# Gated mix of linear attention and a squared-ReLU layer: the query weights folded in one wide burst instead of two narrow ones

## The chip, the cores and the metric

The kernel runs on one core of a Trainium2 chip. The metric is the time of one execution on the device, in microseconds (us). TensorE (PE in the profile) multiplies matrices out of SBUF into eight PSUM banks of 128 x 512 floats; VectorE (DVE), ScalarE (ACT) and GpSimd (POOL) do the element-wise work; SyncE (SP) issues transfers, as GpSimd and ScalarE also do.

## The reference

2048 tokens of width 512, 32 heads of 16, a hidden layer of 1792. Per head the queries and keys go through a small 16x16 matrix `w_phi` and a pair of softmaxes; the attention is linear; its output is mixed by a gate with that of a feed-forward layer:

```python
pq = einsum("bhsd,hdf->bhsf", q, w_phi)          # pk alike from k
phi_q = concat([softmax(pq), softmax(-pq)], -1)  # phi_k alike
kv  = einsum("bhsf,bhsd->bhfd", phi_k, v)
z   = einsum("bhsf->bhf", phi_k)
num = einsum("bhqf,bhfd->bhqd", phi_q, kv)
den = einsum("bhqf,bhf->bhq", phi_q, z)[..., None] + 1e-6
a   = (num / den).transpose(...) @ wo
b   = relu(x @ w1 + b1) ** 2 @ w2 + b2
out = g * a + (1 - g) * b                        # g = sigmoid(sum(x * gate_w))
```

## The kernel before

Every large product is made of three TensorE instructions (`mm3`, L74 to L78): both operands are split into a high and a low part, and high x high, high x low and low x high are added in one bank. The splits (`split`, L61) are a copy on ScalarE (L63) and a subtraction on VectorE (L66).

The work is a list of 56 items (L848), 28 in each of two sweeps. An item is one of the 7 hidden tiles of a sweep for one of the 4 blocks of 512 tokens: twelve products "up" (tile `u`, first layer, into one bank), ScalarE's and VectorE's work on it (`hidden`, L422: relu L425, square L427, split into `hh` and `hl`), and twelve products "down" into four banks `d0` to `d3`, which hold a block's sums over seven items and are then read by VectorE (`gated`, L449). The up of an item is issued two items ahead of its down. The first sweep's partial outputs go to DRAM on GpSimd's queue (L910).

Between these products stands everything else, at places given by slots (`at`, L790): an item has two slots, and half slots lie in the middle of its up and its down. In the first sweep eight pairs of key and value chunks are worked (`pair_steps`, L660, at slot 14 + 4.5 p for pair p): products `pX` and `pY` (L656 to L658), read by ScalarE (L675) and VectorE (L677), the softmaxes (`exps`, L300), and at last the sums over tokens (`kv_chunk`, L323), bursts of small products into the bank `kvps`, which holds them from the first pair to the last. In the second sweep the queries are projected (`do_q`), made into features (`q_phi`, L340), turned and placed by transfers (`transposed`, L361: L363 and L372), and multiplied with the sums (`numer`, L384, `num`) and with `wo` (`attended`, `att`).

Besides `d0` to `d3` there are four banks (`ps_a`, `ps_b`, `ps_e`, `ps_f`). `bank` (L53) hands them out in turn to `u`, `pY`, the folds and the query phase; `ps_b` is out of the turn while it is `kvps`, and `ps_e` while it is `pX`.

The small matrix `w_phi` is not applied to queries but to the weights: `query_fold` multiplies the query weights by it on the chip. The weights come transposed (`wqT`, four rows of 128 x 512, `load_fold`, L141), the small matrices as 32x32 blocks of two heads. `query_fold(half)` (L191) runs at slots 51.5 and 53, near the end of the first sweep: 32 products of a 32x32 block with 128 columns into two banks (64 records in the trace, two to a product). VectorE turns each bank in 32x32 squares (L174) into the tile `turned`, and ScalarE and VectorE split it into `wqh` and `wql`, which `q` (from slot 56.5) reads. The same is done for the keys at the start, with four banks in one burst (`tiles_fold`, L177).

The framework sets each engine's order from the order of the code and from priorities (`high_priority`) and explicit orders (`issue_after`). Within an engine instructions run in that order, and an instruction that waits holds up what is behind it.

## Time and profile before

| | |
|---|---|
| time, median of 3 runs | 506.5 us (506.25 to 506.56) |
| profiled execution | 506.27 us, of which the span of its instructions is 504.5 us |
| PE busy | 499.7 us, 99% of the span |
| VectorE, ScalarE, GpSimd busy | 404.7, 259.9 and 88.1 us |
| mean granted clock of TensorE | 0.999 |
| data moved | 76.13 MB, 151 GB/s on average |

How to read it: times in rows of a timeline are the start, in us from the start of the span, and the duration; "x4" groups instructions that follow each other. Products on PE overlap: a row of 0.39 us is followed by the next start 0.23 us later, so a stretch of PE is measured from start to start. In brackets stands the idle time of the engine ahead of an instruction, with what ended it. Names are those of the program, without buffer numbers: `d`, `u`, `fold`, `num`, `pX`, `pY`, `kvps` are banks.

### The profile page before, as it was taken

To read this page: it belongs to the slowest core of one execution; us is meant where nothing else is said; L and a number is where in the kernel's file an instruction comes from. 1 tells how busy PE (TensorE), PEld (TensorE's weight loads), DVE (VectorE), ACT (ScalarE), POOL (GpSimd) and SP (SyncE) were. 2 spreads that over 40 slices of the span, in tenths; PEclk is the share of its full clock that TensorE was granted. 3 is DMA by queue.
4 is the path that set the end of the run, shared out by engine and by line. 5 is a ranking of instruction groups with operands and counts; after the bars stand their busy time and mean duration, and the time that the engine had idled before them with its cause. 6 is when DMAs were issued, how large, how long until landed. Compare 5 with 4: busy or idle time off the path is not lost.

```text
span 504.5 us, 9559 instructions
## 1 busy us (share of the span) xinstructions
PE 499.7 (99%) x3616; PEld 403.9 (80%) x3616; DVE 404.7 (80%) x680; ACT 259.9 (52%) x470; POOL 88.1 (17%) x103
## 2 busy tenths in 40 slices
PE   8999999999999999999999999999999999999997
PEld 5878788888888888888788878788787878788776
DVE  5569957799785969796988989897979796897724
ACT  4887655466263474453793644454455353333540
POOL 1000151204510025000012140212222221112200
PEclk9999999999999999999999999999999999999999
DMA  8858587666854578762167131324212221041112
GB/s 263 285 197 279 184 315 215 215 216 233 295 187 156 180 225 309 261 218 75 43 182 280 39 109 47 101 71 138 54 31 90 71 88 44 6 136 51 36 29 83
DMA packets 45830, 76.13 MB, mean 151 GB/s; under 512 B 6869, under 2 KB 23001, under 8 KB 45785
## 3 DMA queue, kind: packets, MB, share of 16 engines
q1 hardware_dynamic: 36072, 41.78, 26.5%
q10 hardware_dynamic: 6768, 23.79, 13.6%
q0 software_dynamic: 2944, 9.96, 5.4%
q8 instruction: 28, 0.46, 0.3%
q14 instruction: 18, 0.14, 0.1%
HBM read 57.68 MB, written 11.54 MB: 137 GB/s over the span
## 4 chain that ended last, share of the span: by engine, by line
PE 93%; DMA 3%; DVE 2%; issue 1%; ACT 1%; SPq 0%; ACTq 0%; DVEq 0%
PE d L76 9%; PE d L77 9%; PE d L78 9%; PE u L76 9%; PE u L77 9%; PE u L78 9%; PE pX L656 3%; PE q L78 3%; PE att L78 3%; PE att L76 3%; PE q L76 3%; PE att L77 3%; PE q L77 3%; PE pX L658 3%; PE pX L657 3%; PE pY L656 2%
## 5 line engine op out<-in xcount | busy, mean ns | idle before, releaser
L425 ACT ACTIVATE r<-u,b1c 128x512 f32<-128x512 f32 x56 | 38.5, 687 | 110.1 <-PE u L78 108.3
L76 PE MATMUL d<-w2h,hh 128*128 128x512 f32 x222 | 86.8, 391 | 0.0
L77 PE MATMUL d<-w2l,hh 128*128 128x512 f32 x222 | 86.4, 389 | 0.0
L78 PE MATMUL d<-w2h,hl 128*128 128x512 f32 x222 | 86.4, 389 | 0.0
L76 PE MATMUL u<-xh,w1h 128*128 128x512 f32 x212 | 83.5, 394 | 0.0
L77 PE MATMUL u<-xl,w1h 128*128 128x512 f32 x212 | 82.6, 390 | 0.0
L78 PE MATMUL u<-xh,w1l 128*128 128x512 f32 x212 | 82.5, 389 | 0.0
L337 POOL TENSOR_TENSOR ez<-e,z 128x512 f32<-128x512 f32 x32 | 43.0, 1366 | 164.1 <-ACT e L313 164.1
L66 DVE TENSOR_TENSOR hl<-r,hh 128x512 fp32r<-128x512 f32 x56 | 37.9, 677 | 22.9 <-ACT hh L63 22.9
L76 PEld LDWEIGHTS d<-w2h,hh 128*128 128x128 f32 x222 | 41.7, 188 | 9.6 <-issue 1.0
L76 PEld LDWEIGHTS u<-xh,w1h 128*128 128x128 f32 x212 | 39.8, 188 | 11.4 <-issue 2.9
L78 PEld LDWEIGHTS d<-w2h,hl 128*128 128x128 f32 x222 | 41.7, 188 | 8.7
L77 PEld LDWEIGHTS d<-w2l,hh 128*128 128x128 f32 x222 | 41.7, 188 | 8.5
L78 PEld LDWEIGHTS u<-xh,w1l 128*128 128x128 f32 x212 | 39.8, 188 | 8.4
L77 PEld LDWEIGHTS u<-xl,w1h 128*128 128x128 f32 x212 | 39.8, 188 | 8.0
L313 ACT ACTIVATE e<-e 128x1024 f32<-128x1024 f32 x27 | 28.6, 1060 | 32.5 <-DVE e L311 32.1
L295 DVE TENSOR_REDUCE sm<-e 128x64 f32<-128x1024 f32 x27 | 32.8, 1215 | 10.8 <-ACT e L313 10.8
L63 ACT ACTIVATE hh<-r 128x512 fp32r<-128x512 f32 x56 | 35.1, 627 | 1.0
L427 ACT ACTIVATE r<-r 128x512 f32<-128x512 f32 x56 | 34.9, 624 | 0.7
L378 ACT ACTIVATE phiT<-tb 32x256 f32<-32x256 f32 x64 | 26.4, 413 | 8.8 <-DVE tb L363 7.9
L695 ACT ACTIVATE tmp<-pX 128x512 f32<-128x512 f32 x24 | 14.4, 598 | 29.7 <-PE pX L658 24.7
L347 DVE TENSOR_REDUCE dz<-ez 128x64 f32<-128x1024 f32 x16 | 19.4, 1212 | 11.7 <-POOL ez L337 11.7
(181 smaller groups left out, 981.4 us busy)
## 6 DMA issues: line engine op xcount, KB each, us to landing
sloto<-wkeep ACTq DMA_DIRECT2D x30, 512.0 KB, 4.3
in<-in_xT SPq DMA_DIRECT2D x42, 256.0 KB, 4.4
slotez<-wkeep ACTq DMA_DIRECT2D x15, 512.0 KB, 6.0
phiT<-tb SPq DMA_DIRECT2D x192, 32.0 KB, 1.8
in<-in_w SPq DMA_DIRECT2D x23, 256.0 KB, 3.3
part<-row POOLq DMA_DIRECT2D x16, 256.0 KB, 5.2
row<-part SPq DMA_DIRECT2D x16, 256.0 KB, 3.2
out<-row SPq DMA_DIRECT2D x15, 256.0 KB, 2.2
```

Source lines behind the costliest of these rows:

```text
L63: i = nc.scalar.activation(hi, src, AF.Copy)
L66: st["lo"] = elo.tensor_tensor(lo, src, hi.bitcast(F32), ALU.subtract)
L76: nc.tensor.matmul(o, ah[:, sa], bh[:, sb], start=first, stop=False)
L77: nc.tensor.matmul(o, ah[:, sa], bl[:, sb], start=False, stop=False)
L78: return nc.tensor.matmul(o, al[:, sa], bh[:, sb], start=False, stop=last)
L295: nc.vector.tensor_reduce(sm, e3, AX.X, ALU.add)
L313: nc.scalar.activation(ef, ef, AF.Exp)
L337: nc.gpsimd.tensor_tensor(ez[:, hs, :], e3[:, hs, :], zbc[half], ALU.mult)
L378: nc.scalar.activation(dst, src, AF.Copy)
L425: st["relu"] = nc.scalar.activation(r, ps, AF.Relu, bias=b1c[:, fc:fc + 1])
L427: nc.scalar.activation(r, r, AF.Square)
L656: nc.tensor.matmul(ps, h, wh, start=first and j == 0, stop=False, skip_group_check=True)
```

## The change

`query_fold` runs once, at slot 49.5, with all four banks: sixteen products of a 32x32 block with 512 columns, one for each pair of row group r (which has its own bank) and column group g. Its weights are loaded from slot 46. ScalarE copies the four banks to two tiles `cp` in eight instructions, VectorE turns each `cp` at once (128 x 1024), and sixteen transfers of 32 x 512 put the head groups where the splits want them (tiles `wq`), eight on SyncE's queue and eight on GpSimd's. The splits (`query_split`) follow at slots 52 and 52.5.

So that four banks are free by then, the sums of keys and values are cut in two: pairs 0 to 6 are read out at slot 48.5 (`kv_most`) by four ScalarE copies and `ps_b` goes back into the turn; pair 7 gets a bank of its own, its last products of `pY` come half a slot earlier, its sums a slot earlier, and GpSimd adds the two parts (`kv_done`). The sums and the rows made from them lie in tiles of the value phase that are no longer used. `kv_most` also sets a flag by which the split of one hidden tile gets a high priority. In the query phase the low parts of one block of x move from VectorE to GpSimd, and the work of the first pair gets priority.

```diff
-    def query_fold(half):
-        pss = {r: bank(f"fold{r}") for r in (2 * half, 2 * half + 1)}
-        for g, c, r in [(g, c, r) for g in range(NK) for c in range(4) for r in pss]:
...
-        part_ = lambda t: t.rearrange("p (g r f) -> p g r f", g=NK, f=32)[:, :, 2 * half:2 * half + 2, :]
+    def query_fold():
+        pss = [bank(f"fold{r}") for r in range(4)]
+        wph, *t = st["wT"]
+        for g in range(NK):
+            for r in range(4):
+                rows, cols = slice(32 * r, 32 * r + 32), slice(32 * g, 32 * g + 32)
...
+                        t[g][rows, :].rearrange("p (k c q) -> p c k q", c=4, q=32),
+                        start=True, stop=True, skip_group_check=True)
+        piece = lambda u, nm: work.tile([P, 2 * D], F32, tag=f"o{u}", name=nm, bufs=1)
+        part_ = lambda t: t.rearrange("p (c k r q) -> p c k r q", c=2, k=NK, q=32)
+        cps = [piece(u, "cp") for u in range(2)]
+        for u, cp in enumerate(cps):
+            for r in range(4):
+                with tc.high_priority(offset=AHEAD):
+                    nc.scalar.activation(
+                        part_(cp)[:, :, :, r, :],
+                        pss[r][:, 256 * u:256 * u + 256].rearrange("p (c k q) -> p c k q", c=2, q=32), AF.Copy)
+        tbs = [work.tile([P, 2 * D], F32, tag="tb", name="turned", bufs=2) for _ in range(2)]
+        for cp, tb in zip(cps, tbs):
+            with tc.high_priority(offset=AHEAD):
+                nc.vector.transpose(tb, cp)
+        st["wq"] = [piece(u, "wq") for u in range(2)]
+        for u, w in enumerate(st["wq"]):
+            for c in range(4):
+                for g in range(2):
+                    (nc.sync, nc.gpsimd)[c % 2].dma_start(
+                        w[32 * c:32 * c + 32, 512 * g:512 * g + 512],
+                        tbs[c // 2][32 * (2 * u + g):32 * (2 * u + g) + 32, 512 * (c % 2):512 * (c % 2) + 512])
+
+    def query_split(u):
+        part_ = lambda t: t.rearrange("p (g x) -> p g x", g=NK)[:, 2 * u:2 * u + 2, :]
         for k in range(NK):
-            if not half:
+            if not u:
                 st.setdefault("wa", []).append(tuple(
                     wpool.tile([P, 512], F32R, tag=f"wa{hl}{k}", name=f"wq{hl}{k}") for hl in "hl"))
             hi, lo = st["wa"][k]
-            split(tb[:, :, :, k].rearrange("p r g q -> p g r q"), part_(hi), part_(lo), nc.scalar, nc.vector)
+            src = st["wq"][u].rearrange("p (g k x) -> p g k x", g=2, k=NK)[:, :, k, :]
+            split(src, part_(hi), part_(lo), nc.scalar, nc.vector)
...
         hh = work.tile([P, SB], F32R, tag="hh", name="hh", bufs=LAG + 1)
         hl = work.tile([P, SB], F32R, tag="hl", name="hl", bufs=LAG + 1)
-        st["act"] = split(r, hh, hl, nc.scalar, nc.vector)
+        with tc.high_priority(offset=AHEAD) if st.pop("hurry", False) else nullcontext():
+            st["act"] = split(r, hh, hl, nc.scalar, nc.vector)
...
-            later = kv_chunk(p == 0, False, st["kv"], v["phi", m], v["v", m])
+            elif p == LASTP:
+                st["kv"] = bank("kvps")[:, :2 * P]
-                st["up"] = kv_chunk(False, p == LASTP, st["kv"], v["phi", n], v["v", n])
+                st["up"] = kv_chunk(False, p >= LASTP - 1, st["kv"], v["phi", n], v["v", n])
-        for off, i in zip((0, 1, 1.5, 2, 2.5, 3, 4), (1, 2, 6, 5, 7, 3, 4)):
+        for off, i in zip((0, 1, 1.5, 2, 2.5, 3, 4 - (p == LASTP) / 2), (1, 2, 6, 5, 7, 3, 4)):
-            at(s + 4, banks.append, ps_e)
+            at(s + 3.5, banks.append, ps_e)
-        at(s + 7.5 + (p == LASTP) * 1.5, kv)
+        at(s + 7.5 + (p == LASTP), kv)
...
+        with tc.high_priority(offset=AHEAD) if n < 2 else nullcontext():
+            phi = q_phi(n)
+            if c % 2 == 0:
+                st["pt", n // 2] = work.tile([P, 2, 4, NG, 32], F32, tag="phiT", name="phiT", bufs=1)
+            st["diag", n] = transposed(phi, st["pt", n // 2], c % 2)
...
+    def kv_most():
+        st["hurry"] = True
+        st["kvs"], st["kvt"] = vext[1][:, :2 * P], vext[1][:, 2 * P:4 * P]
+        for s in KV:
+            with tc.high_priority(offset=AHEAD):
+                nc.scalar.activation(st["kvs"][s, :], st["kv"][s, :], AF.Copy)
+        banks.append(ps_b)
...
+        for s in KV:
             with tc.high_priority(offset=AHEAD):
-                nc.scalar.activation(kvs[s, :], kvps[s, :], AF.Copy)
+                nc.scalar.activation(st["kvt"][s, :], st["kv"][s, :], AF.Copy)
+            nc.gpsimd.tensor_tensor(kvs[s, :], st["kvt"][s, :], kvs[s, :], ALU.add)
-        banks.append(ps_b)
...
-    at(49, do_wT, wqT)
-    at(51.5, query_fold, 0)
-    at(53, query_fold, 1)
+    at(46, do_wT, wqT)
+    at(48.5, kv_most)
+    at(49.5, query_fold)
+    for u in range(2):
+        at(52 + u / 2, query_split, u)
```

(`load_x` with an `after` splits its low parts on GpSimd; `q_exps` of n = 1 and 2 are issued behind an instruction of the chunk before; `kv_blocks` behind the last `wql`.)

On PE, around the new fold, from the last product of the up of the fourth block's sixth hidden tile. Numbers tell tiles of one name apart; line numbers are those of each kernel. Before, the four d of this item had pY between them, and no fold:

```order
L78 MATMUL u_2628<-xh3_3_1329,w1l5_347 128x512
L76 MATMUL d0_2349<-w2h3_268,hh_2496 128x512
...
L78 MATMUL d1_2350<-w2h3_268,hl_2497 128x512
L656 MATMUL pY_2619<-w40_766,xh4_2_2086 128x512 [waits DVE_49]
...
L658 MATMUL pY_2619<-w41_770,xl4_3_2104 128x512
L76 MATMUL d2_2351<-w2h3_268,hh_2496 128x512
```

And now:

```order
L78 MATMUL u_2638<-xh3_3_1329,w1l5_347 128x512
L688 MATMUL pY_2629<-w40_766,xh4_2_2086 128x512 [waits DVE_49]
...
L690 MATMUL pY_2629<-w41_770,xl4_3_2104 128x512
L76 MATMUL d0_2349<-w2h3_268,hh_2496 128x512
...
L78 MATMUL d1_2350<-w2h3_268,hl_2497 128x512
L199 MATMUL fold0_2784<-row_2551,row_2550 32x512 [waits Activation_49]
L199 MATMUL fold1_2785<-row_2551,row_2550 32x512 [waits PE_49]
L199 MATMUL fold2_2786<-row_2551,row_2550 32x512 [waits DVE_49,PE_49]
L199 MATMUL fold3_2787<-row_2551,row_2550 32x512
...
L199 MATMUL fold3_2787<-row_2554,row_2550 32x512
L76 MATMUL d2_2351<-w2h3_268,hh_2496 128x512
```

pY's six products stand ahead of those into d0 and d1 and no longer behind, and the sixteen products of the fold come between d1 and d2; its third product is the first one that waits for VectorE. The two bursts that stood later on PE are gone.

On VectorE, the instructions around the two reads of that pY (into `e` and into `vext`), before:

```order
L311 TENSOR_TENSOR tmp_390<-tmp_390,mx_2712 128x32x16 [waits DVE_49]
L66 TENSOR_TENSOR hl_2738<-r_2734,hh_2737 128x512 [waits Activation_49]
L270 SCALAR_TENSOR_TENSOR row_2548,gate_99<-row_2548,gwb_97 128x512 [waits DMAHW3_49,DMASW0_49]
L677 TENSOR_TENSOR e_2709<-tmp_390,pY_2619 128x16x16 [waits PE_49]
L677 TENSOR_TENSOR vext0_107<-tmp_390,pY_2619 128x16x16
```

And now:

```order
L341 TENSOR_TENSOR tmp_390<-tmp_390,mx_2722 128x32x16 [waits DVE_49]
L709 TENSOR_TENSOR e_2719<-tmp_390,pY_2629 128x16x16 [waits PE_49]
L66 TENSOR_TENSOR hl_2752<-r_2748,hh_2751 128x512 [waits Activation_49]
L709 TENSOR_TENSOR vext0_107<-tmp_390,pY_2629 128x16x16
L338 TENSOR_REDUCE mx_2772<-e_2719 128x32 [waits DVE_49]
```

The row of the gate (L270) has moved behind, the read into `e` stands ahead of the split of the hidden tile (`hl`) and the read into `vext` behind it. `pY` and `fold2` share a bank.

On GpSimd, from the last addition of the value phase to the first store of a partial output, before:

```order
L621 TENSOR_TENSOR in_2320<-in_2320,in_2319 128x2x128 [waits Pool_49]
L749 MEMSET row_2823 128x256 [waits DMAHW0_49,DMASW3_49,PE_49]
L910 DMA part_104<-row_3134 128x512 [waits DMASW4_49,DVE_49]
L910 DMA part_104<-row_3138 128x512 [waits DMASW5_49,DVE_49]
L910 DMA part_104<-row_3142 128x512 [waits DVE_49]
```

And now:

```order
L653 TENSOR_TENSOR in_2320<-in_2320,in_2319 128x2x128 [waits Pool_49]
L220 DMA wq_2818<-turned_2814 32x512 [waits DMAHW7_49,DMASW4_49,DVE_49]
L220 DMA wq_2818<-turned_2814 32x512 [waits DMASW5_49]
L220 DMA wq_2818<-turned_2815 32x512 [waits DVE_49]
L220 DMA wq_2818<-turned_2815 32x512
L220 DMA wq_2819<-turned_2814 32x512 [waits DMASW0_49,DMAHW0_49,PE_49,Activation_49]
...
L796 TENSOR_TENSOR vext1_108<-vext1_108 17x256 [waits Activation_49]
L951 DMA part_104<-row_3117 128x512 [waits DMASW4_49,DVE_49]
```

Eight transfers into `wq` stand where a memset stood, and the additions of the two parts of the sums between them and the stores. The other eight transfers stand on SyncE between the row of x for the gate and the loads of weights for the next items.

More of the change, by code (lines that the diff above doesn't have):

```diff
@@ L108, in load_ffn, with load_x @@
         return hi, lo
-    def load_x(b):
+    def load_x(b, after=None):
         xs = []
@@ L115, in load_x @@
             lo = xpool.tile([P, SB], F32R, tag="xl", name=f"xl{b}_{k}")
-            split(t, hi, lo, nc.scalar, nc.vector)
+            with tc.issue_after(after.ins) if after else nullcontext():
+                split(t, hi, lo, nc.scalar, nc.gpsimd if after else nc.vector)
             xs.append((hi, lo))
@@ L189, in tiles_fold @@
                                          tb[:, :, 2 * h:2 * h + 2, k].rearrange("p r g q -> p g r q"), AF.Copy)
-    def query_fold(half):
-        pss = {r: bank(f"fold{r}") for r in (2 * half, 2 * half + 1)}
-        for g, c, r in [(g, c, r) for g in range(NK) for c in range(4) for r in pss]:
-            with tc.issue_after(st["up"].ins):
-                st["up"] = fold_block(st["wT"], pss[r], g, r, c)
-        tb = turned(pss, half)
-        part_ = lambda t: t.rearrange("p (g r f) -> p g r f", g=NK, f=32)[:, :, 2 * half:2 * half + 2, :]
+    def query_fold():
[4 more added lines that the diff above has]
+                rows, cols = slice(32 * r, 32 * r + 32), slice(32 * g, 32 * g + 32)
+                with tc.issue_after(st["up"].ins):
+                    st["up"] = nc.tensor.matmul(
+                        pss[r][cols, :], wph[rows, g * P + 32 * r:g * P + 32 * r + 32],
+                        t[g][rows, :].rearrange("p (k c q) -> p c k q", c=4, q=32),
[20 more added lines that the diff above has]
+                        tbs[c // 2][32 * (2 * u + g):32 * (2 * u + g) + 32, 512 * (c % 2):512 * (c % 2) + 512])
@@ L202, in query_fold @@
             hi, lo = st["wa"][k]
-            split(tb[:, :, :, k].rearrange("p r g q -> p g r q"), part_(hi), part_(lo), nc.scalar, nc.vector)
+            src = st["wq"][u].rearrange("p (g k x) -> p g k x", g=2, k=NK)[:, :, k, :]
+            split(src, part_(hi), part_(lo), nc.scalar, nc.vector)
+        st["wql"] = st["lo"]
     def operand(i, j, src, slot=None, ehi=None, elo=None):
@@ L332, in q_exps @@
     def q_exps(n, ps):
-        e3, r = exps(ps, late=n == 3)
+        with tc.issue_after(st["den" if n == 1 else "tb"].ins) if n in (1, 2) else nullcontext():
+            e3, r = exps(ps, late=n == 3)
         ez = work.tile([P, 2 * H, DH], F32, tag="ez", name="ez", bufs=1)
@@ L362, in transposed @@
         tb = work.tile([P, 2 * D], F32, tag="tb", name="tb", bufs=2)
-        nc.vector.transpose(tb, phi)
+        st["tb"] = nc.vector.transpose(tb, phi)
         later = []
@@ L736, in do_phi @@
     def do_phi(b, n, c):
-        phi = q_phi(n)
-        if c % 2 == 0:
-            st["pt", n // 2] = work.tile([P, 2, 4, NG, 32], F32, tag="phiT", name="phiT", bufs=1)
-        st["diag", n] = transposed(phi, st["pt", n // 2], c % 2)
+        with tc.high_priority(offset=AHEAD) if n < 2 else nullcontext():
[3 more added lines that the diff above has]
+            st["diag", n] = transposed(phi, st["pt", n // 2], c % 2)
         st.setdefault("pieces0" if n % 2 else "", st["pieces"])
@@ L744, in do_n @@
         st["o", pair] = numer(st["pt", pair])
-    def kv_room():
-        t = row()
-        st["kvs"], st["kvt"] = t[:, :2 * P], t[:, 2 * P:]
-        nc.gpsimd.memset(st["kvs"], 0.0)
+    KV = [slice(32 * j, 32 * j + VW) for j in range(4)]
+    def kv_most():
[5 more added lines that the diff above has]
+        banks.append(ps_b)
     def kv_done():
-        kvps, kvs = st["kv"], st["kvs"]
-        for j in range(4):
-            s = slice(32 * j, 32 * j + VW)
+        kvs = st["kvs"]
+        for s in KV:
             with tc.high_priority(offset=AHEAD):
-                nc.scalar.activation(kvs[s, :], kvps[s, :], AF.Copy)
+                nc.scalar.activation(st["kvt"][s, :], st["kv"][s, :], AF.Copy)
+            nc.gpsimd.tensor_tensor(kvs[s, :], st["kvt"][s, :], kvs[s, :], ALU.add)
         nc.sync.dma_start(zrow.rearrange("(j x) -> j x", j=4), kvs[DH::32, :])
         for half in range(2):
-            z = hold.tile([P, H * VW], F32, tag="vz", name=f"z{half}")[:, :D]
+            z = vext[2 * half][:, :D]
             nc.sync.dma_start(z, zrow[half * D:(half + 1) * D].partition_broadcast(P))
             zbc.append(z.rearrange("p (h f) -> p h f", f=DH))
-        banks.append(ps_b)
     def kv_blocks():
-        nc.vector.transpose(st["kvt"], st["kvs"])
+        with tc.issue_after(st["wql"].ins):
+            nc.vector.transpose(st["kvt"], st["kvs"])
         kt = st["kvt"].rearrange("p (g v) -> p g v", v=32)
@@ L826, in tile_gated_mix @@
             at(slot + 1.5, ffn_split, nm, NFH + i)
-    at(51, kv_room)
     at(NB * SL - 1, kv_done)
```

7 lines of the change are left out of this document (4 added, 3 removed).

## The prediction

> **What bounds the kernel now.** I read the page first, then busy time by stretches, then the timelines around the two folds. The page gives TensorE nearly the whole span:
>
> ```profile
> PE 499.7 (99%) x3616; PEld 403.9 (80%) x3616; DVE 404.7 (80%) x680; ACT 259.9 (52%) x470; POOL 88.1 (17%) x103
> ```
>
> One stretch from 60 to 490 us (its length, then busy us of PE, PEld, DVE, ACT, POOL) shows that PE never pauses there, at a granted clock of 1.00:
>
> ```profile
> 60.00:490.00 430.00, 430.00 (x3200) 349.70 (x3199) 356.37 (x591) 216.33 (x380) 83.42 (x88) 1.00 0.43 141
> ```
>
> So only two things count: PE work that goes away, and waits that PE gets. The two folds and what follows them on PE:
>
> ```profile
> 240.52 0.39 PE L78 MATMUL d<-w2h,hl 128*128 128x512 f32 x1
> 240.84 1.15 PE L166 MATMUL fold<-row 32*32 32x128 f32 x64
> 241.92 0.50 PE L76 MATMUL d<-w2h,hh 128*128 128x512 f32 x1
> 242.26 0.39 PE L77 MATMUL d<-w2l,hh 128*128 128x512 f32 x1
> 242.49 0.39 PE L78 MATMUL d<-w2h,hl 128*128 128x512 f32 x1
> ...
> 246.23 1.15 PE L166 MATMUL fold<-row 32*32 32x128 f32 x64
> 247.32 0.50 PE L76 MATMUL d<-w2h,hh 128*128 128x512 f32 x1
> ```
>
> Undisturbed, products start 0.227 apart (L77 to L78). From the L78 ahead of the burst to the L78 behind it are 242.49 − 240.52 = 1.97; three products explain 0.68. A fold therefore costs 1.29, the second one the same (its first follower again comes 1.09 behind its start): 2.58 together.
>
> **The change part by part.** *The burst.* It goes from two bursts of 64 records to one of 32, of 512 columns, over sixteen 32x32 tiles instead of eight. Its price comes from three bursts that are there: num (256 columns, eight tiles), the key fold at the start (128 columns, sixteen tiles) and the groups' mean ns of one record.
>
> ```profile
> 296.59 1.09 PE L389 MATMUL num<-phiT,kvb 64*32 64x256 f32 x32
> ```
> ```profile
> 26.61 1.90 PE L166 MATMUL fold<-row 32*32 32x128 f32 x128
> ```
> ```profile
> L389 PE MATMUL num<-phiT,kvb 64*32 64x256 f32 x256 | 8.8, 382 | 0.0
> L166 PE MATMUL fold<-row 32*32 32x128 f32 x256 | 4.2, 275 | 0.0
> ```
>
> 128 more columns cost 382 − 275 = 107 ns, so a tile takes a 256-column record every 0.214 and a 512-column one every 0.428, which lasts 0.382 + 0.214 = 0.596. Check on num: four turns of eight, 3 x 0.214 + 0.382 = 1.02, and 0.07 for the eight starts make 1.09. The new burst has two turns of sixteen: 0.428 + 0.596 = 1.02, and the sixteen starts take between 0.07 (num's) and 0.19 (in the key fold 127 starts fill 1.90 − 0.275 = 1.63, so 12.8 ns each, times 15). That is 1.09 to 1.21; I take 1.15, the length of one old burst. Saved: 2.58 − 1.29 = **1.29**, 1.23 to 1.35.
>
> [...]
>
> *The bank that it waits for.* The burst needs four banks at once. Its third product writes the bank of pY, which VectorE must have read. In PE's new order pY's six products stand six earlier, behind u, and the two d products that they pass come just before the fold. The first product after pY before, which is now the first fold's place:
>
> ```profile
> 235.31 0.39 PE L76 MATMUL d<-w2h,hh 128*128 128x512 f32 x1
> ```
>
> The L78 ahead of 235.31 starts at 235.08, and a fold followed its L78 by 0.32 (240.52 to 240.84): the first new record could run at 235.40, the third product at 235.43. pY itself, six products earlier, is done 1.36 before 235.31 and a fill of some 0.2, so by 234.2, and VectorE decides:
>
> ```profile
> 233.88 0.69 DVE L311 TENSOR_TENSOR tmp<-tmp,mx 128x512 f32<-128x512 f32 x1
> 234.84 0.69 DVE L66 TENSOR_TENSOR hl<-r,hh 128x512 fp32r<-128x512 f32 x1 [0.26 <-ACT hh L63]
> 235.45 0.68 DVE L270 SCALAR_TENSOR_TENSOR row<-row,gwb 128x512 f32<-128x512 f32 x1
> ...
> 236.06 0.41 DVE L677 TENSOR_TENSOR e<-tmp,pY 128x256 f32<-128x256 f32 x1
> 236.40 0.41 DVE L677 TENSOR_TENSOR vext<-tmp,pY 128x256 f32<-128x256 f32 x1
> ...
> 240.65 1.21 DVE L318 TENSOR_TENSOR tmp<-tmp,r 128x1024 f32<-128x1024 f32 x1
> ```
>
> Now the read into e comes behind L311, from 234.48 to 234.82, in what was idle; then hl, which still waits for ScalarE's hh and starts at 234.84; then the read into vext, at 235.45, done at 235.86. With a few hundredths until PE starts, the third product runs at 235.90: a wait of **0.47** that was not there. Its ends: 0.40 if PE starts at once, 0.65 if ScalarE is late by the 0.2 that the next step allows. Behind the waiting product stand the rest of the burst and every later product; nothing on PE can pass it.
>
> *kv_most.* Four copies on ScalarE after the burst of pair 6, and ahead of two copies of pX:
>
> ```profile
> 228.51 1.29 PE L327 MATMUL kvps<-e,vext 128*17 128x32 f32 x128
> ```
> ```profile
> 231.43 0.39 ACT L675 ACTIVATE tmp<-pX 128x256 f32<-128x256 f32 x1 [5.83 <-PE pX L658]
> ```
> ```profile
> L756 ACT ACTIVATE row<-kvps 17x256 f32<-17x256 f32 x4 | 1.5, 372 | 0.0
> L620 POOL TENSOR_TENSOR in<-in 128x256 f32<-128x256 f32 x7 | 6.4, 909 | 0.6
> ```
>
> They run from 229.8 to 231.3 in ScalarE's 5.83 of idle time: nothing, with 0.1 to spare; what they overrun is added to VectorE's chain above (the 0.2). The four additions of kv_done on GpSimd (0.91 each, four rows like L620) come behind copies that no longer wait for a burst in slot 55; the last puts some 0.9 ahead of kv_blocks, where VectorE had 1.57 of idle time:
>
> ```profile
> 257.40 0.45 DVE L765 STREAM_TRANSPOSE row<-row 128x256 f32<-128x256 f32 x1 [1.57 <-issue]
> ```
>
> *From the banks to the query weights.* The burst ends at 237.05; ScalarE's eight copies (0.39 like L675) take 3.1, until 240.2. The next u stands six d products behind the burst (1.36, so at 238.4) and needs the first bank, which ScalarE's first two copies empty by 237.8: it fits, by 0.6. VectorE's L318 ended at 241.86 and now comes 0.95 earlier, as the read into vext does; the two turns follow it, and then eight transfers on SyncE and eight on GpSimd.
>
> ```profile
> L363 DVE STREAM_TRANSPOSE tb<-e 128x1024 f32<-128x1024 f32 x16 | 19.9, 1241 | 0.3
> ```
> ```profile
> L372 SPq DMA_DIRECT2D phiT<-tb x192: 507/589/1118, 279.3 to 484.4; - x192
> ...
> DMA to landing us min/median/max: 1.8/1.8/5.4
> ```
> ```profile
> L910 POOL DMA_DIRECT2D part<-row x16: 542/543/577, 60.2 to 263.5; - x16
> ...
> DMA to landing us min/median/max: 2.0/3.6/7.8
> ```
>
> The turns end at 242.1 and 243.4. Two transfers of each queue can go after the first, six after the second: SyncE's last is issued by 243.4 + 6 x 0.59 = 246.9 and lands 1.8 later, at 248.7; GpSimd's by 246.7, landing at 250.3 with its median of 3.6. SyncE's next weight loads stand behind these eight and leave some 4 us later. What is due first behind the last piece is in ScalarE's queue: the second set of wqh copies, then the rest up to hh of the last hidden tile, VectorE's read of the d bank, and the next block's first d:
>
> ```profile
> 250.87 1.34 ACT L63 ACTIVATE wqh<-turned 128x256 fp32r<-128x256 f32 x4 [0.38 <-DVE rest L278]
> ```
> ```profile
> 260.48 2.72 DVE L449 SCALAR_TENSOR_TENSOR row<-d,rest,row 128x512 f32<-128x512 f32 x4
> ```
> ```profile
> 262.50 0.39 PE L76 MATMUL d<-w2h,hh 128*128 128x512 f32 x1
> ```
>
> Before, the set started at 250.87, the first read ended at 261.2 and d came 1.3 later. PE will be 0.8 earlier, so the last piece may land until 250.87 + 1.3 − 0.8 = 251.4: 1.1 to spare, cost nothing.
>
> *The query phase.* Low parts of one x block go to GpSimd, and pair 0's chain gets priority. Before, three xl instructions (0.6 each) stood ahead of the second transposition, whose placements end just before num at 296.59:
>
> ```profile
> 282.88 0.69 DVE L66 TENSOR_TENSOR xl<-in,xh 128x512 fp32r<-128x512 f32 x1
> ```
> ```profile
> 279.32 15.39 SPq L372 DMA_DIRECT2D phiT<-tb x24
> ```
>
> The chain gains 1.8, PE only 0.8: nothing.
>
> *Sum.* 506.27 of the profiled execution (span 504.5, the rest lies around it) − 1.29 + 0.47 = 505.45. The median of the runs, 506.5, is 0.23 above it: **505.7**. A measurement of this kernel tells 0.2%, 1.0 us, from no change: faster is below 505.5, slower above 507.5.
>
> **The rivals.** *No wait on the bank* (0.16): both reads are done by 235.43. Then 506.5 − 1.29 = 505.2. For it: e is read in idle time, and an instruction between is all that is in the way. Against it: that instruction, hl, waits for hh until 234.81.
>
> *Sixteen tiles don't run side by side* (0.10): the only burst so far on all sixteen lasts 1.90. At that length it costs 0.75 more: 506.5. Against it: that one had four times the records, and 12.8 ns per start explain it.
>
> *GpSimd's pieces come late* (0.09), the slower side: it decides when the last lands after 251.4, 4.7 behind its issue; from 6.6 on the time is above 507.5. At the row's longest, 7.8, it lands at 254.5, PE waits 3.1 at d, and the time is 508.8. For it: that queue's landings spread from 2.0 to 7.8. Against: those moved 256 KB, these 64 KB.
>
> *VectorE holds GpSimd's transfers up* (0.03): VectorE has work without a pause from the second turn to the first wql, nine instructions of 404.7 / 680 = 0.60 on average, so until 248.8, and there it stops for the pieces itself. If GpSimd could issue only then, eight of 0.543 end at 253.1 and land, at 1.8, at 254.9: a wait of 3.5, 509.2. Against it: GpSimd's sixteen issues all took 542 to 577 ns, with VectorE 80% busy. [...]
>
> **How the numbers follow.** The forecast has 0.62, at 505.7; with the saving of 1.23 to 1.35 and the wait of 0.40 to 0.65 it spans 505.5 to 505.9, and 0.2 either way for the offset of profile and median puts a fifth of it below 505.5. Faster: 0.16 + 0.13 = 0.29. Slower: 0.06 of the late pieces and 0.03: 0.09. The same: 0.62. The range goes from 505.1 (no wait, the largest saving) to 506.8 (the wide burst with the longer wait, and the lightly late pieces): it leaves out a tenth to a fifth.
>
> **What would show it.** In the profile after: one fold burst of 32 records, its first records near 235.4, a gap or a stretch of 0.5 in it, released by VectorE's vext read, and d again 0.23 apart behind it; no other wait of PE until the end; q some 0.8 earlier than 258.42 would confirm the sum. A burst of 1.6 without a named wait would be both together. I am wrong on the mechanism if the burst begins with all its banks free, if a tile's record of 512 columns takes well over 0.6, or if a wait of PE for wql, d or u stands between 238 and 263.

## The result and the profile after

The change made the kernel slower: 514.84 us (513.67 to 515.07) against 506.53 (506.25 to 507.06) for the kernel before on the same chip, a ratio of 1.0158 (1.0141 to 1.0176). The forecast was 505.7, the same. One later run, of e4, took 555.5 at a granted clock of 0.85 and is in no figure below.

The page's line of busy time, after:

```profile
PE 502.5 (98%) x3520; PEld 403.8 (79%) x3520; DVE 405.6 (79%) x674; ACT 262.9 (51%) x482; POOL 98.2 (19%) x118
```

There are 96 records fewer (128 of the narrow bursts gone, 32 of the wide one added), yet PE is busy for longer, over a span of 513.1. The waits of PE (line, releaser, us, times, longest) show where it stopped:

```profile
PE num L420 <- DMA phiT<-tb: 2.7, 1, 2.7
PE num L420 <- ACT phiT L409: 2.1, 1, 2.1
PE warm L525 <- DVE zeros L519: 1.2, 1, 1.2
PE pX L688 <- DMA sloto<-wkeep: 0.6, 1, 0.6
```

Both new waits are at `num` of the query phase, not at the fold. To place the 8.3 us I took the start of each `d` product in both traces; between neighbouring ones the difference moves only where something happened. It is +1.49 by 212 us, +1.07 behind the fold (247 us before), +8.29 behind `num` (299 us before), and stays there. So the fold gained 0.42 and `num` lost 7.2. Of the first +1.49, 0.9 comes up at 106 us, where PE waits for `sloto`, and the rest in smaller steps from 28 us on; PE's order there is that of before, and in other kernels below with the same stretch the difference is −0.5 to +1.1. It was not pursued and stays open.

The fold on PE:

```profile
236.58 0.39 PE L78 MATMUL d<-w2h,hl 128*128 128x512 f32 x1
236.90 2.02 PE L199 MATMUL fold<-row 32*32 32x512 f32 x32
238.85 0.50 PE L76 MATMUL d<-w2h,hh 128*128 128x512 f32 x1
239.19 0.39 PE L77 MATMUL d<-w2l,hh 128*128 128x512 f32 x1
239.42 0.40 PE L78 MATMUL d<-w2h,hl 128*128 128x512 f32 x1
```

From L78 to L78 2.84, less 0.68 for three products: 2.16, against 2.58 for the two narrow ones. VectorE's reads of pY beside it:

```profile
235.99 0.41 DVE L709 TENSOR_TENSOR e<-tmp,pY 128x256 f32<-128x256 f32 x1
236.34 0.69 DVE L66 TENSOR_TENSOR hl<-r,hh 128x512 fp32r<-128x512 f32 x1
236.95 0.41 DVE L709 TENSOR_TENSOR vext<-tmp,pY 128x256 f32<-128x256 f32 x1
```

The read into `vext` ends at 237.36, `hl` stands between the reads, and the burst that began at 236.90 is stretched. Then `num`, and the granted clock (after the busy us of PE, PEld, DVE, ACT, POOL) in two stretches:

```profile
299.83 1.03 PE L420 MATMUL num<-phiT,kvb 64*32 64x256 f32 x2 [2.11 <-ACT phiT L409]
303.51 1.96 PE L420 MATMUL num<-phiT,kvb 64*32 64x256 f32 x30 [2.65 <-DMA phiT<-tb]
305.40 0.80 PE L76 MATMUL u<-xh,w1h 128*128 128x512 f32 x1
306.00 0.63 PE L77 MATMUL u<-xl,w1h 128*128 128x512 f32 x1
```
```profile
300.00:310.00 10.00, 7.34 (x50) 4.54 (x49) 9.15 (x17) 4.67 (x9) 3.23 (x3) 0.67 0.37 121
310.00:350.00 40.00, 40.00 (x205) 32.50 (x204) 37.05 (x60) 18.04 (x35) 5.68 (x5) 1.00 0.26 75
```

Of the 7.2, 4.76 are the two waits; the other 2.4 are products at the lower clock behind them (the burst 1.96 instead of 1.09, its followers 0.80 and 0.63 instead of 0.50 and 0.40). The granted clock was still 1.00 from 299.0 to 299.6 and then 0.50 from 299.7 to 306.5.

What `num` waits for is the end of a chain. The queries come in chunks of 128 tokens. VectorE turns a chunk's features (`tb`; called the chunk's turn below), and the pieces then go into `phiT`, four by copies on ScalarE and twelve by transfers on SyncE (the placements). The first `num` needs a pair of chunks: two turns and 24 placements. Its first wait ended with ScalarE's last copies, the second, which ended later and so decides, with the last placement. The rows along the chain, engine by engine (GpSimd, VectorE, SyncE), each late against before:

```profile
255.34 3.34 POOL L796 TENSOR_TENSOR vext<-vext 17x256 f32<-17x256 f32 x4 [7.37 <-ACT vext L795]
271.63 2.54 POOL L368 TENSOR_TENSOR ez<-e,vext 128x512 f32<-128x512 f32 x2 [6.03 <-DMA in<-in_xT]
286.11 5.49 POOL L66 TENSOR_TENSOR xl<-in,xh 128x512 fp32r<-128x512 f32 x4 [1.05 <-ACT xh L63]
```
```profile
258.70 0.45 DVE L805 STREAM_TRANSPOSE vext<-vext 128x256 f32<-128x256 f32 x1 [3.04 <-POOL vext L796]
289.22 1.17 DVE L382 SCALAR_TENSOR_TENSOR den<-dz 128x32 f32<-128x32 f32 x1
293.19 1.25 DVE L394 STREAM_TRANSPOSE tb<-e 128x1024 f32<-128x1024 f32 x1
```
```profile
264.64 0.83 SPq L800 DMA_DIRECT2D vext<-zrow  x2
282.14 19.80 SPq L403 DMA_DIRECT2D phiT<-tb  x24
```

GpSimd's additions end at 258.68 and VectorE stands 3.04 for them; before, that transposition of the sums (`kv_blocks`) was at 257.40. The sums `z` leave SyncE at 264.64 (before 260.88) and land some 7.1 after their issue, so `ez` starts at 271.63 (before 267.98). The row names another load for this wait; that it was for `z` follows from these times, and in e4, below, the same wait is put down to `z`. Later a `den` takes 1.17 beside GpSimd's four subtractions, and the second turn ends at 294.44 (before 287.20). The last of the 24 placements is issued by 301.94 (before 294.71).

### The profile page after: what moved, and what is told of

It reads as the page before. It is cut to its first block, busy times and chain, and to the rows that moved or that the text cites. A ratio compares the mean times of both kernels' runs of the same rounds, so it can differ in the third digit from the quotient of the medians.

```text
span 513.1 us, 9416 instructions
## 1 busy us (share of the span) xinstructions
PE 502.5 (98%) x3520; PEld 403.8 (79%) x3520; DVE 405.6 (79%) x674; ACT 262.9 (51%) x482; POOL 98.2 (19%) x118
## 4 chain that ended last, share of the span: by engine, by line
PE 80%; DMA 6%; DVE 6%; ACT 2%; SPq 2%; issue 2%; POOL 1%; DVEq 0%; POOLq 0%; ACTq 0%
PE d L76 8%; PE u L76 8%; PE d L77 8%; PE d L78 8%; PE u L77 8%; PE u L78 8%; PE pX L688 3%; PE att L78 3%; PE att L77 3%; PE att L76 3%; PE pX L690 3%; PE pX L689 3%; PE q L78 2%; PE q L77 2%; PE q L76 2%; DMA in<-in_xT 2%
## 5 line engine op out<-in xcount | busy, mean ns | idle before, releaser
L78 PE MATMUL d<-w2h,hl 128*128 128x512 f32 x222 | 86.4, 389 | 0.0
L78 PE MATMUL u<-xh,w1l 128*128 128x512 f32 x212 | 82.6, 390 | 0.0
L368 POOL TENSOR_TENSOR ez<-e,vext 128x512 f32<-128x512 f32 x32 | 42.6, 1353 | 164.7 <-ACT e L343 158.6
L78 PEld LDWEIGHTS d<-w2h,hl 128*128 128x128 f32 x222 | 41.7, 188 | 8.7
L78 PEld LDWEIGHTS u<-xh,w1l 128*128 128x128 f32 x212 | 39.9, 188 | 8.6 <-DVE w1l L66 0.2
```

Of the source, the lines that this page charges most:

```text
L78: return nc.tensor.matmul(o, al[:, sa], bh[:, sb], start=False, stop=last)
L368: st["ez"] = nc.gpsimd.tensor_tensor(ez[:, hs, :], e3[:, hs, :], zbc[half], ALU.mult)
```

## The experiments

Each result is the median with its range in us, then the ratio to the kernel before with its 95% interval. The kernel before, on the same chips, had medians of 506.1 to 506.8. Edits are against the changed kernel unless it is said otherwise.

**Which part costs it.** e1 takes the three query edits out of the changed kernel; e2 puts them alone into the kernel before.

```diff
-        with tc.issue_after(st["den" if n == 1 else "tb"].ins) if n in (1, 2) else nullcontext():
-            e3, r = exps(ps, late=n == 3)
+        e3, r = exps(ps, late=n == 3)
...
-            st["x", b] = load_x(b % NB, st["ez"] if b == NB + 1 else None)
+            st["x", b] = load_x(b % NB)
...
-        with tc.high_priority(offset=AHEAD) if n < 2 else nullcontext():
-            phi = q_phi(n)
+        phi = q_phi(n)
```

> The changed kernel with the edits of the query phase undone: low parts of the x block on VectorE again, no order behind den or the transposition for the exponentials of chunks 1 and 2, no priority for the first pair's chain. The wide fold and the split sums stay. The wait at the first num (2.1 + 2.65 us, then a slow clock; 7.2 us by the d products' starts) is what the whole loss consists of. Theory Z (the rows of z come late, since the additions on GpSimd hold VectorE and through it SyncE's queue): the wait stays in part, 1.5 to 3 us, time 508.5 to 511. Theory Q (the query edits themselves make the chain late): no wait at num, time about 506 (506.5 less the 0.4 that the fold gained).

> The kernel before with only the edits of the query phase: low parts of one x block on GpSimd, the exponentials of chunks 1 and 2 behind den and the transposition of chunk 0 and 1, priority for the first pair. Two narrow folds and the undivided sums stay. Theory Q: the wait at num is there without the fold, 3 us or more, time 510 to 514. Theory Z: z is in time here, so no wait or one under 1 us, time 506 to 507.5.

e1: 512.18 (510.62 to 512.99), 1.0102 (1.0082 to 1.0122); PE still waits 3.5 at `num`. e2: 509.99 (508.88 to 511.43), 1.0064 (1.0042 to 1.0086), a wait of 2.0 and none of the fold's parts in it. Neither time lies in a range that was expected. So there are two losses, one from the query edits (some 3) and one, the larger, from the fold's side (some 5).

**Which query edit.** e3 and e4 put back one line each of the diff above (x on VectorE; no order of the exponents); e6 is e2 with x on VectorE.

> The changed kernel with only the low parts of the x block back on VectorE. Four small VectorE instructions took 0.82 to 1.31 us beside GpSimd's four subtractions, instead of 0.2 to 0.7. Theory P (the two engines hold each other up at SBUF): those four get back to 0.2 to 0.7, the second transposition comes 1 to 3 us earlier, time 511 to 513.5. If the long durations have another cause (the clock, waits within), they stay, and the time does not fall.

> The changed kernel without the order that puts the exponentials of chunk 1 behind den of chunk 0 (and those of chunk 2 behind a transposition). Theory O (that order, on top of late z rows, makes chunk 1 late): the exponentials of chunk 1 run in VectorE's 3.4 us of idle time before 274.2, the wait at num shrinks by 3 us or more, time 507 to 510. Theory Z alone: chunk 1 still waits for z, the wait shrinks by under 1.5 us, time 512.5 to 514.

> As e2 (the kernel before with the query edits), but the low parts of the x block stay on VectorE. In e2 the wait at num was 2.0 us, and VectorE's dz, den, hl and the gate's product took 0.69, 1.19, 1.83 and 0.89 us beside GpSimd's subtractions. Theory P: without GpSimd at work there they take 0.2, 0.2, 0.7 and 0.25, no wait is left at num, time 506.3 to 507.3. If the order of the exponentials is what makes the chain late, the wait stays at 1.5 us or more, time 509 to 510.5.

e3: 512.94 (512.76 to 514.66), 1.0130 (1.0109 to 1.0151): the four small instructions are back at 0.19 to 0.63 and the second turn ends at 292.61 instead of 294.44, as expected, though the interval overlaps that of the changed kernel (1.0141 to 1.0176). e4: 511.74 (511.33 to 512.38), 1.0098 (1.0082 to 1.0115): the second turn ends at 291.73, and the time is clearly below the changed kernel's, between the two that were expected. So the order of the exponents costs in the changed kernel too. e6: 507.37 (506.70 to 508.38), 1.0028 (1.0016 to 1.0040), with a wait of only 0.25 left at `num`. So by the medians some 1.8 of e2's 3.2 is the four subtractions on GpSimd; the two intervals barely part. VectorE's second chunk in e2, beside them (281.78 to 287.28), and in e6, without them:

```profile
282.48 0.69 DVE L350 TENSOR_TENSOR dz<-dz,r 128x64 f32<-128x64 f32 x1
283.20 1.19 DVE L353 SCALAR_TENSOR_TENSOR den<-dz 128x32 f32<-128x32 f32 x1
284.31 1.83 DVE L66 TENSOR_TENSOR hl<-r,hh 128x512 fp32r<-128x512 f32 x1
286.06 0.34 DVE L354 RECIPROCAL den<-den 128x32 f32<-128x32 f32 x1
```
```profile
282.08 0.23 DVE L350 TENSOR_TENSOR dz<-dz,r 128x64 f32<-128x64 f32 x1
282.34 0.19 DVE L353 SCALAR_TENSOR_TENSOR den<-dz 128x32 f32<-128x32 f32 x1
282.45 0.68 DVE L66 TENSOR_TENSOR hl<-r,hh 128x512 fp32r<-128x512 f32 x1
283.05 0.34 DVE L354 RECIPROCAL den<-den 128x32 f32<-128x32 f32 x1
```

`dz`, `den` and `hl`, whose two inputs are in SBUF, take 0.46, 1.00 and 1.15 more, the reciprocal none. The durations are those of theory P; that the two engines meet at SBUF, as it has it, is not shown.

**z and the bank.** e5 is e1 with `z` on GpSimd's queue; e7 is e5 with `hl` issued behind both reads of pY; e8 is e7 with the two parts of the sums added by VectorE straight from the bank.

```diff
-        nc.sync.dma_start(zrow.rearrange("(j x) -> j x", j=4), kvs[DH::32, :])
+        nc.gpsimd.dma_start(zrow.rearrange("(j x) -> j x", j=4), kvs[DH::32, :])
...
+                    if i == 4 and "late" in st:                       # e7
+                        with tc.issue_after(read.ins):
+                            st["lo"] = st["dve"] = st.pop("late")()
...
-                nc.scalar.activation(st["kvt"][s, :], st["kv"][s, :], AF.Copy)
-            nc.gpsimd.tensor_tensor(kvs[s, :], st["kvt"][s, :], kvs[s, :], ALU.add)
+                nc.vector.tensor_tensor(kvs[s, :], st["kv"][s, :], kvs[s, :], ALU.add)   # e8
```

> As e1 (the wide fold and the split sums, no query edits), but the three transfers of z go out on GpSimd's queue, right behind its additions, instead of SyncE's, where they stood behind loads of wo and w2 that wait for VectorE. In e1 the first ez started at 271.09 and the second transposition at 290.53, and the loss at num was 5.65 us by the d products' starts. Theory Z: ez starts at 267 to 268.5 again, the second transposition at 285.5 to 287.5, the loss at num is under 1 us, time 506 to 507.5. If something else on the chain is late (the q products, VectorE's order), the loss stays above 3 us and the time above 510.

> As e5, and the low part of the hidden tile (hl) is issued behind both reads of pY's bank, instead of between them. In the changed kernel the fold's third product started 0.60 us late, behind the read into vext, and the next twelve another 0.28 later; the burst lasted 2.02. Theory B (the wait on that bank is what the burst has over 1.15): it lasts 1.05 to 1.2, PE gains 0.8 to 0.9 on e5, time 505.2 to 506.3. If sixteen wide products take about 2 us in any case, the burst stays at 1.9 to 2.0 and the time is that of e5.

> As e7, and the two parts of the sums are added by VectorE straight out of the bank (four instructions) instead of a ScalarE copy and a GpSimd addition each. In the changed kernel VectorE sat idle for 3.04 us for the last of these additions, with the splits of wo behind it. Theory Z goes on: z is ready some 2 us earlier still; if e7 has no wait at num left, this brings nothing more: within 0.3 us of e7. If e7 still waits at num, it is 1 us or more faster than e7.

e5: 512.34 (510.19 to 513.04), 1.0119 (1.0097 to 1.0140); `z` is in time (`ez` starts at 270.16, right behind Exp), but ScalarE stands 3.55 for a load of `w2` ahead of the first Exp (269.03, before 266.83), and the loss stays. e7: 513.97 (513.61 to 515.35), 1.0161 (1.0146 to 1.0176). e8: 514.45 (514.09 to 515.00), 1.0168 (1.0155 to 1.0182). Both were expected below 506.3 and lose at `num` even more: their first Exp comes later still (269.98 and 270.44; in e8 ScalarE stands 2.89 and 3.73 for loads of `w2`), and why these loads are later was not tested. But their burst is the one to read, here e8's:

```profile
234.99 0.39 PE L78 MATMUL d<-w2h,hl 128*128 128x512 f32 x1
235.31 1.30 PE L199 MATMUL fold<-row 32*32 32x512 f32 x32
236.53 0.50 PE L76 MATMUL d<-w2h,hh 128*128 128x512 f32 x1
236.87 0.39 PE L77 MATMUL d<-w2l,hh 128*128 128x512 f32 x1
237.10 0.40 PE L78 MATMUL d<-w2h,hl 128*128 128x512 f32 x1
```

From L78 to L78 2.11, less 0.68: 1.43. So the wide burst without a bank to wait for costs 1.43, and the wait in the changed kernel 2.16 − 1.43 = 0.73. It is not chance: in the seven kernels here with `hl` behind both reads the burst lasts 1.29 to 1.39, in the nine with the wide fold and `hl` between them 1.93 to 2.05.

**The late loads.** e9 is e5 with the `kv_blocks` turn behind chunk 0's exponents on VectorE and the split of w2's last piece behind chunk 0's Exp; e10 is e9 with e7's order; e11 is the changed kernel with e9's two orders.

```diff
-        with behind():
+        with behind(), tc.issue_after(st["exp"].ins) if (nm, fc) == ("w2", NF - 1) else nullcontext():
...
-        with tc.issue_after(st["wql"].ins):
+        with tc.issue_after(st["ex"].ins):
```

> As e5, with two orders changed: the turn of the sums (kv_blocks) comes behind the first q chunk's exponents on VectorE, so that VectorE does not stop for GpSimd's additions with the splits of wo behind it; and the split of the last w2 tile comes behind the first chunk's exponential on ScalarE. In e5 z was in time, but ScalarE stood 3.55 us for a load of w2 (w2h12) with the exponential behind it (269.03, before 266.83). Theory L (weights loaded late, behind buffers that VectorE frees late, hold ScalarE ahead of the exponential): the exponential starts at 266.5 to 267.5, the first ez at 267.7 to 268.7, no wait over 1 us at num, time 505.3 to 506.8. If the chain is late in VectorE's later part in any case, the wait stays at 2 us or more and the time is above 509.

> As e9, and hl behind both reads of pY's bank as in e7. Theories L and B together: no wait at num, none at the fold, a burst of 1.05 to 1.4 us, time 0.6 to 0.8 below e9, 504.7 to 505.9, which is 0.6 to 1.3 below the kernel before. If the wait at num stays, 509 or more.

> The changed kernel with the two orders of e9 only: z still goes out on SyncE, the low parts of the x block stay on GpSimd, the query edits stay, the bank of pY is still waited for. Theory L with P: the exponential is in time, z comes earlier since SyncE's loads do, but GpSimd's subtractions still hold VectorE up as in e2, so a wait of 1.5 to 3 us at num is left, time 508 to 510.5. If the query edits do no harm once the loads are in time, 505.8 to 507.

e9: 512.66 (511.65 to 512.98), 1.0115 (1.0101 to 1.0130). e10: 514.20 (512.40 to 515.04), 1.0141 (1.0123 to 1.0160). e11: 514.84 (513.10 to 516.38), 1.0150 (1.0128 to 1.0173). All three miss their forecasts: e9's first Exp is back at 266.74 (before 266.83), and the wait stays at 3.5. So late loads were not the whole cause. In e11, which leaves `z` on SyncE, Exp comes at 267.34 and `ez` only at 271.71: there `z` alone makes the first turn late (282.35). e9's VectorE shows something else:

```profile
271.59 0.54 DVE L327 RECIPROCAL r<-sm 128x64 f32<-128x64 f32 x1
272.29 0.69 DVE L66 TENSOR_TENSOR w2l<-in,w2h 128x512 fp32r<-128x512 f32 x1 [0.15 <-ACT w2h L63]
272.90 0.68 DVE L338 TENSOR_REDUCE mx<-q 128x32 f32<-128x512 f32 x1
273.50 0.68 DVE L339 TENSOR_REDUCE mn<-q 128x32 f32<-128x512 f32 x1
274.10 0.21 DVE L382 TENSOR_TENSOR dz<-dz,r 128x64 f32<-128x64 f32 x1
```

Between `r` and `dz` of chunk 0 stand a split of w2 and chunk 1's maxima and minima (in the kernel before `dz` followed `r` at 272.26), two more of chunk 1 follow, and the first turn ends 3.4 later than in the kernel before.

**The queue of the placements.** What these kernels have in common stands in their traces. The table has the ends of the two turns on VectorE, the end of the last issue on SyncE, the start of `num`'s last 30 records, and PE's waits at `num`:

| kernel | turn 1 | turn 2 | last issue | num's 30 | waits |
|---|---|---|---|---|---|
| before | 279.26 | 287.20 | 294.71 | 296.6 | 0 |
| after | 282.08 | 294.44 | 301.94 | 303.51 | 4.8 |
| e1 | 283.69 | 291.77 | 299.47 | 301.04 | 3.5 |
| e2 | 277.74 | 290.13 | 297.62 | 299.20 | 2.0 |
| e6 | 277.34 | 287.90 | 295.41 | 296.99 | 0.2 |
| e9 | 282.67 | 290.01 | 298.73 | 300.11 | 3.5 |

The last issue ends 7.5 behind turn 2 (after, e2, e6) or 15.4 to 16.1 behind turn 1 (before, e9), whichever is later: 12 or 24 transfers at 0.63 to 0.67 in one queue. In the 14 kernels that have all placements on SyncE and where PE paused there, the 30 records begin 1.37 to 1.58 behind that end (in e16, below, with two queues, 1.84). e12 sets VectorE's order right in e9 (the two query edits other than x); e13 is e9 with six of the second chunk's twelve placements on GpSimd; e14 is both with e7's order; e15 puts the six on GpSimd in the kernel before.

```diff
-                    st["pieces"] = nc.sync.dma_start(dst, src)
+                    st["pieces"] = (nc.gpsimd if two and r % 2 else nc.sync).dma_start(dst, src)
```

(`two` is n == 1.)

> e9 with the two edits of the query chain that it lacked: chunk 1's exponents stand behind chunk 0's den, and the first two chunks' multipliers and turns go ahead (the low halves of x stay on VectorE). In e9 VectorE did four operations of chunk 1 between r (271.59) and dz (274.10) of chunk 0, so that the first turn ended at 282.67 (before: 279.26). Theory Q (the 24 placements of both chunks stand in one queue on SyncE at 0.64 each, and num waits until first turn + 15.4 + 1.83, or second turn + 7.6 + 1.83, whichever is later): the first turn ends near 277.5, the second near 288, the last placement lands near 297.4, PE waits under 1 at num and its clock stays at 1.0: 506.5 (505.8 to 507.5). Rival W (the late loads of w2 hold ScalarE and VectorE, whatever the order): a wait of 2 or more stays, 510 or more.

> e9 with six of the second chunk's twelve placements on GpSimd's queue instead of SyncE's; the chain of the chunks stays as late as in e9 (first turn 282.67, second 290.01). Theory Q: SyncE issues 18 x 0.64 = 11.5 from 282.75, or 6 x 0.63 from 290.0, so the last lands near 296.1 instead of 299.97; PE, which comes to num at 296.7, does not wait, and the slower products after the pause (0.43 and 0.72 instead of 0.23, some 3 us in all) go with the wait: 506.7 (505.9 to 507.7). Rival W: not the queue but VectorE's and ScalarE's lateness is waited for; a wait of 2 or more stays, 510 or more.

> e12 and e13 together, and hl issued behind both reads of the pY bank (e7's edit), which is the changed kernel with its wide burst and with every wait taken off that the runs have shown. Theory Q: no wait at the burst, none at num; the burst's gain of 1.1 stays to the end: 505.4 (504.8 to 506.2). Rival: something of the kept late work (w2's load at 268, GpSimd's additions) still reaches PE at num or behind it: 506.5 or more.

> The kernel before with the same six placements on GpSimd's queue and nothing else. In it the 24th placement is issued by 294.71 and lands near 296.55, and PE starts num at 296.59 with no wait shown. Theory Q: nothing to take away, 506.5 (506.2 to 506.9). Rival (PE's arrival is itself held by the queue, or the split is worth something by itself): 505.8 or less; GpSimd's issues hold VectorE: over 507.

e13: 508.71 (508.44 to 509.43), 1.0045 (1.0030 to 1.0059). Its placements on SyncE and on GpSimd, and `num`:

```profile
282.28 12.25 SPq L406 DMA_DIRECT2D phiT<-tb  x18
```
```profile
290.12 2.99 POOL L406 DMA_DIRECT2D phiT<-tb  x6 [11.28 <-issue]
```
```profile
295.86 1.48 PE L423 MATMUL num<-phiT,kvb 64*32 64x256 f32 x32
```

The chain is as late as in e9 (the first turn ends at 282.21), the queue is done at 294.53 instead of 298.73, and PE does not wait at `num`. The time falls by some 4 but not to the 506.7 that was expected, since PE then waits at `att`:

```profile
305.04 0.51 PE L78 MATMUL att<-woh,o 128*128 128x512 f32 x1 [1.58 <-DVE o L66]
```

By the starts of the `d` products e9 loses 6.8 at `num`, e13 0.4 there and 1.9 at `att`. e15: 506.38 (505.36 to 507.87), 0.9995 (0.9982 to 1.0008): as a control, the split is worth nothing by itself. e12: 512.01 (511.15 to 512.85), 1.0105 (1.0087 to 1.0123): turn 1 came to 279.75, turn 2 only to 290.65, the wait to 2.1, and a new one of 1.9 stands at the first products of `att`. e14: 513.06 (512.57 to 513.98), 1.0128 (1.0109 to 1.0146): nothing at `num`, 1.0 and 3.6 at `att`. Both times were missed. Both kernels hold chunk 2's exponents back, which may make `o` late; but e13 waits for `o` without that hold, so this cause is not shown.

**Back to the old times.** e16 has e14's cures without the hold on chunk 2 and without raised priority, w2's last load ahead of SyncE's loads of partial rows, and no order for that piece's split; e17 is e16 with all placements on SyncE; e18 is e16 with w2's last split behind Exp again and `kv_blocks` behind chunk 1's exponents.

```diff
-            nc.sync.dma_start(st["f", n], part[n])
+            with tc.issue_after(st["last"].ins):
+                nc.sync.dma_start(st["f", n], part[n])
```

> The changed kernel with its wide burst, and the query chain brought back to the times that it had before: x split on VectorE, chunk 1's exponents behind chunk 0's den (chunk 2's not held), no raised priority, z over GpSimd's queue, the kv_blocks turn behind chunk 0's exponents, SyncE's loads of partial rows behind the last load of w2 (in e9 and e13 that load stood behind them and came at 268.4, and w2's split made VectorE wait inside the chain), hl issued behind both reads of the pY bank, and six of the second chunk's placements on GpSimd. Theory Q: first turn near 279, second near 287, the last placement lands near 293, the third chunk's products on GpSimd start by 291.5, so neither num nor the first attention products wait, and the burst's gain of 1.1 stays: 505.4 (504.9 to 506.2). Rival: the additions on GpSimd, with the turn of the sums that stands in the chain, still cost: a wait of 1 or more at num or at the attention products, 506.5 or more.

> As e16, but with all 24 placements on SyncE. Theory Q: the last lands near 279 + 15.4 + 1.84 = 296.3 and PE, earlier by the burst's gain, comes to num near 295.6: a wait of some 0.6, so the queue keeps half of the gain: 505.9 (505.3 to 506.7), between before and e16. Rival: 506.5 or more, or no difference from e16.

> e16 with two more orders: the split of the last piece of w2 stands behind chunk 0's Exp on ScalarE (in e16 ScalarE stood 4.04 for that piece and Exp came at 269.52, where before has 266.83), and the kv_blocks turn and its copies stand behind chunk 1's exponents. Theory Q (num waits on the chain of the chunks and on the queue of their placements, nothing else): Exp near 266.8, first turn near 279.3, second near 287, the third chunk's products on GpSimd by 292, no wait over 0.3 at num or at the attention products: 505.4 (504.8 to 506.3), the first version below before. Rival (each cure uncovers another wait, since ScalarE, VectorE and the stage buffers of this stretch are full with the fold's work standing 2 later than before): 507 or more, with a wait of 1 or more left.

e16: 511.98 (511.85 to 513.26), 1.0123 (1.0104 to 1.0141). e17: 514.59 (514.49 to 515.23), 1.0169 (1.0153 to 1.0184). Both miss. In both ScalarE stood 4.0 to 4.7 for that load ahead of Exp (269.52 and 270.15), and the turns ended 4 to 6 late; PE waited 2.0 at `num` in e16, 5.5 in e17 with its single queue. So the late loads are a cause after all, beside VectorE's order. e18: 508.48 (507.59 to 509.44), 1.0044 (1.0029 to 1.0059). Its turns end at 280.05 and 287.86, near the 279.3 and 287 that were expected, nothing waits at `num`, and PE is there 1.5 earlier than in the kernel before; the time of 505.4 is missed all the same. What follows (PE; VectorE):

```profile
301.96 0.39 PE L77 MATMUL att<-wol,o 128*128 128x512 f32 x1
304.45 0.50 PE L78 MATMUL att<-woh,o 128*128 128x512 f32 x1 [2.10 <-DVE o L66]
```
```profile
300.34 2.20 DVE L354 TENSOR_TENSOR e<-e,w 128x1024 f32<-128x1024 f32 x1
302.57 1.25 DVE L400 STREAM_TRANSPOSE tb<-e 128x1024 f32<-128x1024 f32 x1
303.74 1.25 DVE L66 TENSOR_TENSOR o<-num,o 128x512 fp32r<-128x512 f32 x2
```

The same three in the kernel before:

```profile
299.81 1.22 DVE L318 TENSOR_TENSOR e<-e,w 128x1024 f32<-128x1024 f32 x1
301.06 1.25 DVE L363 STREAM_TRANSPOSE tb<-e 128x1024 f32<-128x1024 f32 x1
302.23 1.25 DVE L66 TENSOR_TENSOR o<-num,o 128x512 fp32r<-128x512 f32 x2
```

`o` stands behind chunk 2's chain on VectorE. Its first half was done near 302.8 in the kernel before, and the product that reads it ran at 303.64: 0.8 of slack. In e18 PE came 1.5 earlier, the product of `e` and `w` started 0.5 later and took 1.0 longer beside GpSimd's `ez` (in e13 it takes the same 2.20), and the wait is 2.1. No kernel was faster than the one before beyond its interval.

## Why the prediction was wrong

*The burst.* The step put it at 1.15 (1.09 to 1.21) long and 1.29 in cost; without a wait it is 1.30 long and costs 1.43 (e8). The saving is 1.15, not 1.29: right in kind, mis-sized by 0.14.

*The bank.* The mechanism was right: e8, with `hl` moved and both reads early, has no stretch in its burst. The size was wrong: 0.73 where the step had 0.47 and at most 0.65. VectorE's reads came as foreseen: the one into `vext` ended 0.46 behind the start of the burst, and the weights of the third and fourth product were loaded at 237.48. But those of the last twelve followed only at 237.80, a second pause for which the profile names no releaser and which was not tested. Together the fold gained 0.42 where the sum had 0.82.

*kv_most and the transfers into wq.* Both cost PE nothing at their own places, as said: ScalarE's copies started at 231.35 behind 4.26 of idle time, and PE does not wait between the fold and `num`.

*kv_done.* "The last puts some 0.9 ahead of kv_blocks, where VectorE had 1.57" failed. VectorE stood 3.04 for the additions. The step had not looked at what now stands behind that transposition on VectorE: the second of the four splits of `wo`, which before stood ahead of it. It came 4.5 later (259.07, before 254.55), and SyncE's next loads of `wo` (259.75, before 255.30) and `z` came later too; that stage buffers which came free late passed this on is argued from the order and not tested. The remark that SyncE's loads leave some 4 later was made and not followed to its end.

*The query phase: this is the step that failed.* "The chain gains 1.8, PE only 0.8: nothing." The chain lost 2.8 at the first turn and 7.2 at the second. Several things did it: the late `z` (e11), the late loads ahead of Exp (e5, e16: ScalarE stands 3.6 to 4.0), the order of chunk 1's exponents (held back they make the second turn late, e4; not held back they stand among chunk 0's work and make the first turn late, e9), and the subtractions on GpSimd (e2 against e6). How much of the 7.2 is due to each stays open, since in these runs one lateness takes the place of another. And the price of lateness was at hand: the quoted row of placements ends at 294.71, 1.8 of landing makes 296.5, and `num` began at 296.59. There was almost no slack to spend, so PE paid for the lateness with waits of 4.8, and the lower clock added 2.4. That the SyncE queue is what passes it on to `num` is shown by e13 against e9, with e15 as control.

*The rivals.* Late pieces on GpSimd's queue did not happen; the pieces were in time, and the eight issues took 4.11 in all, 0.51 each, so VectorE did not hold them up either. There was a wait on the bank, and the sixteen tiles do run side by side (1.30, not 1.90). What happened was on no list: a lateness like that of the pieces, one phase further on, behind the last sign of being wrong that was named (263). And even the gain of 1.1 would have met the 0.8 of slack at `att`.

## What to carry to other kernels

When PE is 99% busy, "no wait" need not mean slack: take every chain that ends at a PE instruction and write down by how much it arrives early, before costing an edit upstream at nothing. Work moved to the idlest engine (GpSimd, 17%) can still make a chain late on which the busiest one waits (a wait of 2.0 at `num` in e2, 0.2 in e6, without the subtractions there), and it can stop VectorE (3.04 for the additions). A gain on PE counts only up to the smallest slack of the chains that it then runs into.

## What the runs showed of the hardware

- VectorE's `dz` and `den` go from 0.23 and 0.19 to 0.69 and 1.19 (e2 against e6), in the changed kernel to 1.31 and 1.17, beside GpSimd's subtractions, and 128 x 1024 from 1.22 to 2.20 beside GpSimd's product (e18, where that started 0.18 ahead); reciprocals (0.34) do not change. In the kernel before the same two start within 0.01 of each other, and there it is GpSimd that takes longer: 2.38 instead of 1.30 for the first half of its `ez`, with VectorE's product at 1.22. What sets which of the two is longer is not shown.
- In these runs the length of PE's wait alone does not tell whether the clock falls. In the changed kernel PE's last product ended at 297.72, and from 299.7, 2.0 later, the granted clock was 0.50; in e16 two waits of 0.99 and 1.05 with two products of `num` between them were enough. Single waits of 2.03 to 2.11 (e2, e12, e18) left it at 1.00. The stretches at 0.50 last 3.4 (e4, e16), 6.8 (after, e14) or 10.2 (e11).
- A record of 512 columns on a 32x32 tile lasts 0.587 in the median of the changed kernel (0.596 was worked out), yet two rounds of sixteen take 1.30 (e8), 0.09 above the upper end of the forecast. What fills it is open.
